# The shift of the first score tiles, added by VectorE out of PSUM instead of by ScalarE and GpSimd

## Chip, cores and metric

The kernel runs on one core of one Trainium2 chip. The metric is the device time of one execution in microseconds (us). TensorE does the matrix products, ScalarE (ACT) the exponentials and many copies, VectorE (DVE) and GpSimd (POOL) elementwise work, SyncE (SP) issues the DMAs.

## What is computed

Two independent blocks on 2048 tokens of width 448, side by side in the output:

```python
# block A: real part of a two-dimensional DFT by matrices
a = einsum("bsd,ed->bse", x, dft_hid_re);  b = einsum("bsd,ed->bse", x, dft_hid_im)
yA = einsum("ts,bse->bte", dft_seq_re, a) - einsum("ts,bse->bte", dft_seq_im, b)
# block B: attention with 16 heads of 28
q, k, v = split(x @ wqkv);  p = softmax(q @ k.T * 28**-0.5);  yB = concat_heads(p @ v) @ wo
out = concatenate([yA, yB], axis=-1)
```

All data are float32. Products whose precision matters are done in three parts: each factor is split into a rounded high part (type float32r) and the remainder, the low part, and high × high, low × high and high × low are summed in PSUM.

## The kernel before

**Work.** Block B first projects x to Q, K and V: chains of 11 matmuls (three row blocks of 128 with three products each, and a last one with two), 28 chains for Q and K (`project`, line 622, with 512 columns) and 16 for V (`values`, line 652, with 448). The results go out to DRAM: for Q and K as a high and a low part (`stored`, line 590: ACT copies the high part out of the PSUM bank at line 593, VectorE subtracts the low part at line 594), for V by a VectorE copy (line 667). Block A has two parts, real and imaginary. Each has 16 hidden products (`hidden`, line 678, again chains of 11 matmuls, with the high part copied by ACT at line 689 or 693 and the low part taken by VectorE at line 690 or 695) and 16 sequence products of 192 matmuls (`sequence`, line 700). The matrices for them come in pieces: ACT rounds the high part (line 520), POOL subtracts the low part (line 526).

Attention runs head by head, with keys on the partitions: per head 16 key tiles × 4 chunks of 512 queries. A score matmul (line 862) writes a PSUM bank, ACT takes the exponential into a kept tile (line 866), and after every 8 key tiles one group of products with V (line 844; 32 products, 64 matmul records) adds them up. 

**The shift.** No running maximum is kept. Instead a shift per query is found from the first key tile of each head (`first_tiles`, line 788): four score matmuls (line 800), copied out by ACT (line 804); VectorE transposes them in blocks of 32 (line 805), takes maxima (806 to 820) and leaves the negated shift in `am`, 64 values wide, with the query of a block on the partitions. Then, for each of the four chunks, VectorE transposes `am`, broadcast, into a PSUM bank (line 826). ACT copies that bank to the SBUF tile `mb`, rounded to float32r (line 829). POOL copies one row of `mb` into row 96 of the chunk's Q tile (line 830), so that the score matmuls of the other key tiles add the shift by themselves, and POOL adds `mb` to the first tile's scores (line 832). ACT then takes their exponential (line 834). So every score matmul at line 862 waits for its chunk's row.

**PSUM.** Of the 8 banks, 2 (`fill_s`) serve the chains of projections and of block A; 6 (`bank_s`) serve scores, transposes, the shift and the sums over V.

**Kept tiles.** `kept_s` has 20 pairs (`NKEPT`) of 128 × 512 float32. A pair holds exponentials until their group of products with V has run; the projections' and block A's results pass through pairs too. Three more pairs are lent where the weights of block A are not in use.

**Order.** Every engine executes its instructions in a fixed order, which is planned when the program is written out (`Schedule`, line 173). Each step has a key, roughly the time in us when it is due, the steps it depends on and the buffers it needs. The planner walks through time with its own prices for every step; an engine that is free takes the ready step with the lowest key. The argument `soon` lowers the key:

```python
t.engs, t.key, t.emit, t.lat, t.lock, t.mode = engs, key - soon, emit, lat, lock, mode   # line 188
```

`SOON` is 40. Before, the rounding of a piece (line 520) and the high copy of a hidden product (689, 693) have it; the high copy of a projection (593) has not, and has the key of its chain less 10, while an exponential has the key of its score matmul less 20. The keys of the heads run evenly from 56 to 935 us (`T_ATT`, `T_END`), those of the other matrix work, the filler, evenly to 1005 us (`T_FILL`), and TensorE interleaves the two by key. The first tiles of a head have keys that begin 26 before the head's.

**End.** After the last head's products with V its sums are normalised by way of DRAM (`out_of`, line 873). The output projection (line 984) follows; what is left of the filler covers the time between.

Of the kernel before, what the change touches and what calls it, by code (L numbers as in the profile page):

```python
# [11 lines left out]
F32 = mybir.dt.float32  # L12
F32R = mybir.dt.float32r
AF = mybir.ActivationFunctionType
ALU = mybir.AluOpType
# [9 lines left out]
P = 128  # L25
NT = S // P
CH = 512
# [3 lines left out]
SCALE = DH ** -0.5  # L31

KM = 98
NKEPT = 20
NKEYS = 5
NFILL = 2
Q_YO = 2
# [3 lines left out]
SOON = 40.0  # L41
# [7 lines left out]
def f32(ap):  # L49
    return ap.bitcast(F32)  # L50
# [275 lines left out]
def tile_kernel(ctx, tc, xa, wre, wim, wd, xb, wqkv, wo, out):  # L326
    nc = tc.nc
# [7 lines left out]
    def new(name, shape, dtype=F32, n=None, in_turn=False, space=None):  # L335
        if space is DRAM:
            return dram.tile(shape, dtype, name=name)
        if n is None:
            return sb.tile(shape, dtype, tag=name, name=name)
        sch.pools.append(Slots([sb.tile(shape, dtype, tag=f"{name}{i}", name=f"{name}{i}") for i in range(n)], in_turn))  # L340
        return sch.pools[-1]
# [18 lines left out]
    v_s = new("v", [P, NC, 4, VW], F32, 2, True)  # L360
    q_s = new("q", [P, CH], F32R, 8, True)
    kept_s = new("kept", [P, 2, CH], F32, NKEPT)
    mb_s = new("mb", [P, CH], F32R, 2, True)
    sm_s = new("sm", [P, 2, NT], F32, 2)
    qm_s = new("qm", [P, 4, 4 * NT], F32, 2, True)
    am_s = new("am", [P, 4 * NT], F32, 2, True)
    ok = new("ok", [P, 2 * H], F32)
    banks = [ps.tile([P, CH], F32, tag=f"bank{i}", name=f"bank{i}") for i in range(8)]

# [4 lines left out]
    fill_s, bank_s = Slots(banks[:NFILL]), Slots(banks[NFILL:])  # L374
# [36 lines left out]
    def act(key, emit, d=ACT_P, **kw):  # L411
        return sch.add({"ACT": d}, key, lambda e: emit(), **kw)

    def dve(key, emit, d=DVE_P, **kw):
        return sch.add({"DVE": d}, key, lambda e: emit(), **kw)

    def pool(key, emit, d=POOL_2, **kw):
        return sch.add({"POOL": d}, key, lambda e: emit(), **kw)
# [171 lines left out]
    def stored(j, c, o, end, own, hi, lo, st, key, out_key):  # L590
        cols = slice(c * CH, (c + 1) * CH)
        as_r, as_f = (lambda t: t if st else f32r(t)), (lambda t: f32(t) if st else t)
        a = act(key, lambda: nc.scalar.activation(as_r(hi.t), o.t, AF.Copy), deps=[end], use=[o, *own])
        b = dve(key, lambda: nc.vector.tensor_tensor(as_r(lo.t), o.t, as_f(hi.t), op=ALU.subtract), deps=[a], use=[o, *own])  # L594
        qk_done[j, c] = [
            dma(out_key, lambda: nc.sync.dma_start(f32(qk_d[j * P:(j + 1) * P, 0, cols]), as_f(hi.t)), deps=[a], use=own),
            dma(out_key, lambda: nc.sync.dma_start(f32(qk_d[j * P:(j + 1) * P, 1, cols]), as_f(lo.t)), deps=[b], use=own)]
# [54 lines left out]
    def values(ready, chunks):  # L652
        for c in chunks:
            v_done[c] = []
            for t in range(4):
                tok = slice(c * CH + t * P, c * CH + (t + 1) * P)
                o, pair = fill_s.slot(), kept_s.slot()
                vs = Half(pair, 0)
                seq = products(lambda k: lz(x_h, k, tok), lambda k: lz(x_l, k, tok), lambda: lz(x_3, tok),
                               lambda k: (lambda: w_first.h[:, k]), lambda k: (lambda: w_first.l[:, k]))  # L660
                key = fkey(11, M448)
                end = chain(key, seq, o, D, [], [], M448, [pair],
                            {3 * k: [xb_ready[c, k], ready[k], *ready[4:][:k // 3]] for k in range(4)}, v_last)

                def put(o=o, vs=vs):
                    v3 = vs.t.rearrange("p (h d) -> p h d", h=H)
                    nc.vector.tensor_copy(v3[:, :, :DH], o.t[:, :D].rearrange("p (h d) -> p h d", h=H))
                    nc.vector.memset(v3[:, :, DH:DH + 1], 1.0)
                    nc.vector.memset(v3[:, :, DH + 1:], 0.0)
                b = dve(key - 20, put, 0.85, deps=[end], use=[o, pair])  # L670
                v_done[c].append(dma(key - 20, lambda vs=vs, c=c, t=t: nc.sync.dma_start(
                    v_d[:, :, (4 * c + t) * VW:(4 * c + t + 1) * VW].rearrange("h p x -> p h x"),
                    vs.t.rearrange("p (h x) -> p h x", h=H)), extra=1.0, deps=[b], use=[pair]))
# [83 lines left out]
    KT, VT, Q = {}, {}, {}  # L757
# [27 lines left out]
    R = {}  # L785
    checked = []

    def first_tiles(h):

        qm, am = qm_s.slot(), am_s.slot()  # L790
        Q[h] = [q_s.slot() for c in range(NC)]
        pairs = [kept_s.slot() for _ in range(NC // 2)]
        R[h] = {0: [Half(pairs[c // 2], c % 2) for c in range(NC)]}
        key0 = begins[h] - 26
        made, rs = [], []
        for c in range(NC):
            key = key0 + 2 * c
            q, s, o, tm = Q[h][c], R[h][0][c], bank_s.slot(), bank_s.slot()
            lq = load_q(h, c, q)
            m = pe(key, lambda e, o=o, q=q: nc.tensor.matmul(  # L800
                o.t, KT[h][0].t[:KR, :P], q.t[:KR, :], start=True, stop=True),
                deps=[*lq, *got_k[h, 0], before.get("f")], use=[o, s.pair, q, KT[h][0], tm])
            in_line("f", m)
            made.append(act(key, lambda o=o, s=s: nc.scalar.activation(s.t, o.t, AF.Copy), deps=[m], use=[o, s.pair], lock=[o]))  # L804
            t = dve(key, lambda o=o, tm=tm: nc.vector.transpose(tm.t, o.t), 0.66, deps=[m], use=[o, tm], lock=[o], own=RAW_S)  # L805
            rs.append(dve(key, lambda tm=tm, c=c: nc.vector.tensor_reduce(  # L806
                qm.t[:, 0, c * NT:(c + 1) * NT], tm.t.rearrange("p (j r) -> p j r", r=32), axis=AX.X, op=ALU.max, negate=True),
                0.64, deps=[t], acq=[qm] if c == 0 else [], use=[tm] if c == 0 else [tm, qm], own=RAW_S))
        key = key0 + 8

        def beside(i):
            return lambda: nc.vector.tensor_copy(qm.t[:32, i, :], qm.t[32 * i:32 * i + 32, 0, :])  # L812

        def back(n):
            return lambda: nc.vector.tensor_copy(am.t[n:2 * n, :], am.t[:n, :])
        r = [dve(key, beside(i), SMALL, deps=rs, use=[qm]) for i in (1, 2, 3)]
        r = dve(key, lambda: nc.vector.tensor_reduce(  # L817
            am.t[:32, :], qm.t[:32].rearrange("p i x -> p x i"), axis=AX.X, op=ALU.min), 0.4,
            deps=r, acq=[am], use=[qm])
        for n in (32, 64):  # L820
            r = dve(key, back(n), SMALL, deps=[r], use=[am])
        row, shown = [], []
        for c in range(NC):
            key = key0 + 10 + 2 * c
            q, s, pm, mb = Q[h][c], R[h][0][c], bank_s.slot(), mb_s.slot()
            t = dve(key, lambda pm=pm, c=c: nc.vector.transpose(  # L826
                pm.t, am.t[:, c * NT:(c + 1) * NT].unsqueeze(2).to_broadcast([P, NT, 32])), 0.64,
                deps=[r], acq=[pm], use=[am])
            ld = act(key, lambda pm=pm, mb=mb: nc.scalar.activation(mb.t, pm.t, AF.Copy), deps=[t], acq=[mb], use=[pm])  # L829
            row.append(pool(key, lambda q=q, mb=mb: nc.gpsimd.tensor_copy(q.t[96:97, :], mb.t[96:97, :]), 0.7,  # L830
                            deps=[ld], use=[mb, q]))
            sh = pool(key, lambda s=s, mb=mb: nc.gpsimd.tensor_tensor(s.t, s.t, f32(mb.t), op=ALU.add), deps=[ld, made[c]],  # L832
                      use=[s.pair, mb])
            shown.append(act(key, lambda s=s: nc.scalar.activation(s.t, s.t, AF.Exp, scale=SCALE), ACT_S, deps=[sh], use=[s.pair]))  # L834
        return row, shown

# [62 lines left out]
    o = bank_s.slot()  # L899
# [18 lines left out]
    key = fkey(0, 0)  # L918
    staged = [d for j in range(N_FIRST, 5) for c in range(NC) for d in qk_done[j, c]]
    made = hidden(0, w_first, load_w(w_first, lambda k: wd[:, k, :D], key - 10, after=[v_last[0], *staged]), x_users)  # L920
# [3 lines left out]
    key = fkey(0, 0)  # L924
    w_b = Weights(lent)
    lent.until.append(key - 50)
    made = hidden(1, w_b, load_w(w_b, lambda k: wd[:, k, D:], key - 10, after=[a_last]), [y_last])
# [12 lines left out]
    for n, c in enumerate(range(NC)):  # L940
        raws = []
        for k in range(4):
            pair = kept_s.slot()
            raw = Half(pair, 0)
            key = T_OUT + n
            deps = [o_done[h, c] for h in range(H) if (h + 1) * DH > k * P and h * DH < (k + 1) * P] + [before["k"]]
            if k < 3:
                ld = dma(key, lambda raw=raw, k=k, c=c: nc.sync.dma_start(raw.t, on_d[k * P:(k + 1) * P, c * CH:(c + 1) * CH]),
                         deps=deps, use=[pair])
            else:  # L950
# [3 lines left out]
                ld = dma(key, twice, 128, n=2, deps=deps, use=[pair])  # L954
            raws.append((raw, ld))
        for i in range(2):
            x = [q_s.slot() for _ in range(4)]
            ready = []
            for k in range(4):
                raw, ld = raws[k]  # L960
# [148 lines left out]
```

## Time and profile before

| | us |
|---|---|
| median of 3 runs | 1024.51 (1023.98 to 1025.2) |
| the profiled execution | 1024.84, span 1022.9 |
| TensorE busy | 1010.6 (99%) |
| ACT busy | 742.3 (73%) |
| POOL busy | 405.6 (40%) |
| VectorE busy | 280.5 (27%) |
| granted TensorE clock | 0.999 of full speed |

A row of a group of instructions reads: line, engine, operation, output <- inputs, shapes, count, then busy us, mean ns of one, and the idle time of the engine just before them with what ended it. A row of the timeline reads: start in us, length in us, engine, line, operation, count, and in brackets the idle time before it and its releaser. A row of the chain of waits has start, length and the piece of work. PE is TensorE's matmuls, PEld its weight loads.

### The profile page before, as it was taken

How to read it: one execution, taken by the hardware profiler on the slowest of the kernel's cores; microseconds unless marked ns; L12 is line 12 of the kernel's file. 1: busy time of each engine (PE TensorE's matmuls, PEld its weight loads, DVE VectorE, ACT ScalarE, POOL GpSimd, SP SyncE). 2: the span in 40 equal slices, each digit the busy share in tenths (PEclk: the TensorE clock that was granted, in tenths of full speed). 3: DMA queues.
4: the chain of work that ended last, by engine and by line, in shares of the span. 5: the costliest groups of instructions: out<-in, count | busy, mean ns of one | idle time of the engine just before them, and what ended most of it. 6: DMA issues, size and time to landing. Idle time of an engine off the chain costs nothing.

```text
span 1022.9 us, 16066 instructions
## 1 busy us (share of the span) xinstructions
PE 1010.6 (99%) x5634; PEld 730.5 (71%) x5634; DVE 280.5 (27%) x542; ACT 742.3 (73%) x1471; POOL 405.6 (40%) x410
## 2 busy tenths in 40 slices
PE   8999999999999999999999999999999999999997
PEld 7885667776666676767767776666676767777896
DVE  6351415241403122131313141503113131300212
ACT  6137879878787878686878878787868687977232
POOL 7021332444352525253534535352535253553530
PEclk9999999999999999999999999999999999999999
DMA  9795464314242323333332424233424334243732
GB/s 322 219 164 159 153 198 136 111 51 124 73 123 83 109 88 114 94 103 104 110 105 84 132 84 114 74 113 99 127 94 130 104 110 122 76 136 101 218 126 92
DMA packets 109909, 124.84 MB, mean 122 GB/s; under 512 B 48640, under 2 KB 61440, under 8 KB 109824
## 3 DMA queue, kind: packets, MB, share of 16 engines
q1 hardware_dynamic: 109824, 123.78, 40.5%
q8 instruction: 45, 0.74, 0.3%
q14 instruction: 40, 0.33, 0.1%
HBM read 89.92 MB, written 33.69 MB: 121 GB/s over the span
## 4 chain that ended last, share of the span: by engine, by line
PE 93%; DVE 3%; ACT 2%; DMA 1%; issue 1%; SPq 0%; DVEq 0%; ACTq 0%
PE bank L714 30%; PE bank L844 22%; PE bank L862 22%; PE bank L577 15%; PE bank L984 4%; PE bank L800 1%; ACT kept L866 1%; DVE big L423 1%; DMA kept<-wqkv 1%; DMA kept<-xb 0%; DVE bank L826 0%; DVE qm L812 0%; ACT kept L804 0%; DVE kept L594 0%; DVE am L817 0%
## 5 line engine op out<-in xcount | busy, mean ns | idle before, releaser
L866 ACT ACTIVATE kept<-bank 128x512 f32<-128x512 f32 x958 | 520.0, 670 | 84.1 <-PE bank L862 75.5
L526 POOL TENSOR_TENSOR wlo<-wraw,whi 128x512 fp32r<-128x512 f32 (+1 forms) x164 | 201.8, 1231 | 437.4 <-ACT whi L520 363.9
L862 PE MATMUL bank<-q,k 98*128 98x512 f32 x960 | 339.1, 401 | 1.6 <-ACT kept L866 1.2
L714 PE MATMUL bank<-big,whi 128*128 128x448 f32 x1024 | 316.3, 368 | 0.0
L844 PE MATMUL bank<-kept,v 128*32 128x512 f32 x2044 | 226.4, 594 | 0.0
L862 PEld LDWEIGHTS bank<-q,k 98*128 98x128 f32 x960 | 179.9, 188 | 55.0 <-ACT kept L866 8.5
L714 PEld LDWEIGHTS bank<-big,whi 128*128 128x128 f32 x1024 | 193.1, 189 | 31.1 <-issue 7.5
L714 PE MATMUL bank<-big,wlo 128*128 128x448 f32 x512 | 188.3, 368 | 0.0
L844 PEld LDWEIGHTS bank<-kept,v 128*32 128x32 f32 x2044 | 63.3, 110 | 144.7 <-issue 142.0
L520 ACT ACTIVATE whi<-wraw 128x512 fp32r<-128x512 f32 x164 | 113.9, 695 | 26.9 <-PE bank L714 20.0
L714 PEld LDWEIGHTS bank<-big,wlo 128*128 128x128 f32 x512 | 96.7, 189 | 15.8 <-issue 5.0
L805 DVE STREAM_TRANSPOSE bank<-bank 128x512 f32<-128x512 f32 x64 | 46.7, 730 | 205.3 <-PE bank L800 158.4
L832 POOL TENSOR_TENSOR kept<-kept,mb 128x512 f32<-128x512 f32 x64 | 82.3, 1286 | 5.1
L577 PE MATMUL bank<-wd,whi 128*128 128x448 f32 x256 | 80.3, 367 | 0.8 <-DVE big L690 0.7
L834 ACT ACTIVATE kept<-kept 128x512 f32<-128x512 f32 x64 | 44.5, 701 | 42.5 <-POOL kept L832 42.5
L830 POOL CAST q<-mb 1x512 fp32r<-1x512 f32 x64 | 38.9, 608 | 90.5 <-ACT mb L829 88.1
L804 ACT ACTIVATE kept<-bank 128x512 f32<-128x512 f32 x64 | 41.5, 653 | 42.3 <-PE bank L800 40.8
L577 PE MATMUL bank<-big,whi 128*128 128x512 f32 x175 | 60.1, 396 | 1.5 <-DVE kept L594 1.2
L577 PEld LDWEIGHTS bank<-wd,whi 128*128 128x128 f32 x256 | 48.3, 189 | 7.7 <-DVE big L690 1.1
L772 DVE TENSOR_REDUCE ok<-v 128x1 f32<-128x512 f32 x16 | 11.0, 686 | 141.0 <-DMA v<-vd 141.0
L829 ACT ACTIVATE mb<-bank 128x512 fp32r<-128x512 f32 x64 | 42.3, 723 | 5.6 <-DVE bank L826 5.5
L806 DVE TENSOR_REDUCE qm<-bank 128x16 f32<-128x512 f32 x64 | 44.0, 688 | 1.9
(74 smaller groups left out, 707.4 us busy)
## 6 DMA issues: line engine op xcount, KB each, us to landing
wraw<-wre SPq DMA_DIRECT2D x64, 256.0 KB
wraw<-wim SPq DMA_DIRECT2D x64, 256.0 KB
qkd<-kept SPq DMA_DIRECT2D x40, 256.0 KB
wraw<-xa SPq DMA_DIRECT2D x32, 256.0 KB
k<-qkd SPq DMA_DIRECT2D x64, 112.0 KB
q<-qkd SPq DMA_DIRECT2D x64, 112.0 KB
out<-kept SPq DMA_DIRECT2D x32, 224.0 KB
kept<-xb SPq DMA_DIRECT2D x16, 256.0 KB
```

Source lines behind the costliest of these rows:

```text
L520: a = act(key + (0 if early else 1), lambda: nc.scalar.activation(self.hi.t, raw.t, AF.Copy), ACT_S, soon=SOON, deps=[ld], acq=[self.hi], ...
L526: b = sch.add(e, at, lambda g: eng[g].tensor_tensor(self.lo.t[:, :n], raw.t[:, :n], f32(self.hi.t)[:, :n], op=ALU.subtract), deps=[a], acq ...
L577: nc.tensor.matmul(o.t[:, :cols], w(), x(), start=(i == 0), stop=(i == n - 1))
L714: nc.tensor.matmul(o.t[:, :D], a.t[:, k, :], b[:, q * 4 + k, :], start=(q == 0 and k == 0 and j == 0), stop=(q == 3 and k == 3 and j == 2))
L805: t = dve(key, lambda o=o, tm=tm: nc.vector.transpose(tm.t, o.t), 0.66, deps=[m], use=[o, tm], lock=[o], own=RAW_S)
L806: rs.append(dve(key, lambda tm=tm, c=c: nc.vector.tensor_reduce(qm.t[:, 0, c * NT:(c + 1) * NT], tm.t.rearrange("p (j r) -> p j r", r=32), ...
L829: ld = act(key, lambda pm=pm, mb=mb: nc.scalar.activation(mb.t, pm.t, AF.Copy), deps=[t], acq=[mb], use=[pm])
L832: sh = pool(key, lambda s=s, mb=mb: nc.gpsimd.tensor_tensor(s.t, s.t, f32(mb.t), op=ALU.add), deps=[ld, made[c]], use=[s.pair, mb])
L834: shown.append(act(key, lambda s=s: nc.scalar.activation(s.t, s.t, AF.Exp, scale=SCALE), ACT_S, deps=[sh], use=[s.pair]))
L844: nc.tensor.matmul(o.t[c * VW:(c + 1) * VW, :], VT[h].t[:, kt // 4, kt % 4, :], tiles[kt][c].t, start=(kt == 0), stop=(kt == NT - 1))
L862: m = pe(key, lambda e, o=o, q=q, kt=kt: nc.tensor.matmul(o.t, KT[h][kt // 4].t[:KM, kt % 4 * P:(kt % 4 + 1) * P], q.t[:KM, :], start=True ...
L866: es.append(act(key - 20, lambda o=o, p=p: nc.scalar.activation(p.t, o.t, AF.Exp, scale=SCALE), deps=[m], use=[o, p.pair]))
```

## The change

1. `am` becomes float32r, so the shift is rounded in the 64 wide reduction that makes it. The transposed shift in PSUM needs no rounding copy after that: the ACT copy to `mb`, and `mb` itself, are dropped.
2. The row of Q is copied out of PSUM by VectorE instead of out of `mb` by POOL.
3. The shift is added to the first tile's scores by VectorE, straight from PSUM, instead of by POOL from `mb`.
4. `NKEPT` is 21 instead of 20; `mb` had two tiles of 128 × 512, which is the size of a pair.
5. The high copy of a projection out of its bank gets `soon=SOON`, and the copy of a V projection out of its bank gets a key lower by 25.

```diff
-NKEPT = 20
+NKEPT = 21
...
-    mb_s = new("mb", [P, CH], F32R, 2, True)
...
-    am_s = new("am", [P, 4 * NT], F32, 2, True)
+    am_s = new("am", [P, 4 * NT], F32R, 2, True)
...
-        a = act(key, lambda: nc.scalar.activation(as_r(hi.t), o.t, AF.Copy), deps=[end], use=[o, *own])
+        a = act(key, lambda: nc.scalar.activation(as_r(hi.t), o.t, AF.Copy), deps=[end], use=[o, *own], soon=SOON)
...
-                b = dve(key - 20, put, 0.85, deps=[end], use=[o, pair])
+                b = dve(key - 45, put, 0.85, deps=[end], use=[o, pair])
...
-            q, s, pm, mb = Q[h][c], R[h][0][c], bank_s.slot(), mb_s.slot()
+            q, s, pm = Q[h][c], R[h][0][c], bank_s.slot()
             t = dve(key, lambda pm=pm, c=c: nc.vector.transpose(
-                pm.t, am.t[:, c * NT:(c + 1) * NT].unsqueeze(2).to_broadcast([P, NT, 32])), 0.64,
+                pm.t, f32(am.t)[:, c * NT:(c + 1) * NT].unsqueeze(2).to_broadcast([P, NT, 32])), 0.64,
                 deps=[r], acq=[pm], use=[am])
-            ld = act(key, lambda pm=pm, mb=mb: nc.scalar.activation(mb.t, pm.t, AF.Copy), deps=[t], acq=[mb], use=[pm])
-            row.append(pool(key, lambda q=q, mb=mb: nc.gpsimd.tensor_copy(q.t[96:97, :], mb.t[96:97, :]), 0.7,
-                            deps=[ld], use=[mb, q]))
-            sh = pool(key, lambda s=s, mb=mb: nc.gpsimd.tensor_tensor(s.t, s.t, f32(mb.t), op=ALU.add), deps=[ld, made[c]],
-                      use=[s.pair, mb])
+            row.append(dve(key, lambda q=q, pm=pm: nc.vector.tensor_copy(q.t[96:97, :], pm.t[96:97, :]), 0.55, deps=[t], use=[pm, q]))
+            sh = dve(key, lambda s=s, pm=pm: nc.vector.tensor_tensor(s.t, s.t, pm.t, op=ALU.add), deps=[t, made[c]], use=[s.pair, pm])
```

The numbers 0.64, 0.55 and the like are the planner's prices in us; the add is planned at 0.60.

## The prediction

> **What bounds the kernel now.** I read the page's busy times first, then the stretches, then the chain of waits, then the timeline around each place where TensorE starts a matmul late, and last the groups of instructions for prices.
>
> ```profile
> span 1022.9 us, 16066 instructions
> PE 1010.6 (99%) x5634; PEld 730.5 (71%) x5634; DVE 280.5 (27%) x542; ACT 742.3 (73%) x1471; POOL 405.6 (40%) x410
> ```
>
> TensorE is busy 99% of the span. Of the engines the change touches, ACT has 73%, POOL 40%, VectorE 27%. "Busy" is modelled from pipelined matmuls, so I also want the rate at which they start:
>
> ```profile
> 937.24 0.93 PE bank L862 x4
> 950.62 28.57 PE bank L714 x140
> 979.19 35.90 PE bank L984 x176
> 1015.09 1.45 PE bank L714 x7
> ```
>
> In these pieces of the chain of waits a 448-column matmul costs 28.57/140 = 0.204 us and a 512-column one 0.93/4 = 0.233 us. A matmul that starts later than this after the one in front has lost time, even where the row shows no idle time.
>
> The Trainium skill ("Perfetto Trace Analysis", Identifying the Most-Contended Engine) says that matmul busy time is a poor measure and that weight-load busy time should be used; by its 71% TensorE would have room. The trace does not bear this out here: 147 matmuls of one line run at 0.204 to 0.207 us with no release from another engine between them, so in this program weight loads hide under matmuls.
>
> Where is time lost?
>
> ```profile
> 60.00:310.00 250.00, 247.28 (x1361) 173.09 (x1360) 80.33 (x162) 199.60 (x397) 95.40 (x104) 1.00 0.45 129
> 310.00:600.00 290.00, 289.89 (x1682) 203.20 (x1681) 70.67 (x130) 221.86 (x438) 117.85 (x106) 1.00 0.34 101
> ```
>
> The columns are TensorE, weight load, VectorE, ACT, POOL busy. From 310 to 600 us TensorE stands 0.1 us; from 60 to 310 us it stands 2.7 us, and there ACT is busy 80%. That early stretch has the projections and the first hidden products, whose chains of 11 matmuls alternate between two PSUM banks. So the change can only win what is lost there (and in the second hidden stage near 610 us); elsewhere less work on ACT or POOL is worth nothing. I looked at each late start:
>
> ```profile
> 85.53 4.21 ACT L866 ACTIVATE kept<-bank 128x512 f32<-128x512 f32 x8
> 87.01 3.29 PE L862 MATMUL bank<-q,k 98*128 98x512 f32 x9
> 89.34 0.89 ACT L593 ACTIVATE wd<-bank 128x512 fp32r<-128x512 f32 x1
> 90.33 0.69 DVE L594 TENSOR_TENSOR wd<-bank,wd 128x512 fp32r<-128x512 f32 x1 [10.08 <-ACT wd L593]
> 90.78 0.51 PE L862 MATMUL bank<-q,k 98*128 98x512 f32 x1 [0.48 <-ACT kept L866]
> ...
> 109.33 0.86 PE L862 MATMUL bank<-q,k 98*128 98x512 f32 x3
> 110.42 0.73 PE L577 MATMUL bank<-big,whi 128*128 128x512 f32 x2 [0.23 <-DVE wd L594]
> ...
> 64.72 3.84 PE L577 MATMUL bank<-wd,big 128*128 128x448 f32 x18
> 68.96 1.09 PE L577 MATMUL bank<-wd,big 128*128 128x448 f32 x4 [0.40 <-DVE kept L667]
> ...
> 221.21 1.91 DVE L826 STREAM_TRANSPOSE bank<-am 128x512 f32<-128x512 f32 x3
> 222.33 0.78 PE L577 MATMUL bank<-wd,whi 128*128 128x448 f32 x3
> 223.15 0.63 DVE L690 TENSOR_TENSOR big<-bank,big 128x448 fp32r<-128x448 f32 x1
> 223.83 0.47 PE L577 MATMUL bank<-wd,whi 128*128 128x448 f32 x1 [0.73 <-DVE big L690]
> ...
> 276.66 2.51 DVE L826 STREAM_TRANSPOSE bank<-am 128x512 f32<-128x512 f32 x4
> 277.42 0.60 ACT L829 ACTIVATE mb<-bank 128x512 fp32r<-128x512 f32 x1 [0.49 <-DVE bank L826]
> 277.95 0.37 PE L714 MATMUL bank<-big,whi 128*128 128x448 f32 x1
> 278.15 0.61 POOL L830 CAST q<-mb 1x512 fp32r<-1x512 f32 x1 [2.72 <-ACT mb L829]
> 278.56 0.51 PE L862 MATMUL bank<-q,k 98*128 98x512 f32 x1 [0.24 <-ACT kept L866]
> ...
> 117.97 1.22 PE L862 MATMUL bank<-q,k 98*128 98x512 f32 x3
> 119.02 0.63 PE L577 MATMUL bank<-big,whi 128*128 128x512 f32 x2
> ...
> 616.55 1.44 PE L862 MATMUL bank<-q,k 98*128 98x512 f32 x3
> 617.83 0.37 PE L577 MATMUL bank<-wd,whi 128*128 128x448 f32 x1
> ```
>
> Start to start, less the pitch: (a) 87.01 to 90.78 is 3.77 for nine, less 9 × 0.233 = 2.10: 1.67 lost. TensorE had only score matmuls to run, at the pace of the exps, because the projection bank was not copied out: the copy L593 stood on ACT behind eight exps. (b) 109.33 to 110.42: 1.09 − 0.70 = 0.39, again released by L594 behind L593. (c) 64.72 to 68.96: 4.24 − 18 × 0.204 = 0.57, released by the value copy L667. (d) 222.33 to 223.83: 1.50 − 0.61 = 0.89; the low half L690 stood behind three transposes. (e) 277.95 to 278.56: 0.61 − 0.20 = 0.41; the first score matmul of a head waits for the shift's row to pass VectorE, ACT and POOL. (f) Five more (the first and last are shown: 1.05 − 0.70 = 0.35 and 1.28 − 0.70 = 0.58), where ACT is behind with exps or with copies, 2.2 together. Sum: 1.67 + 0.39 + 0.57 + 0.89 + 0.41 + 2.2 = 6.1 us. That is what there is to win.
>
> **The change part by part.**
>
> ```profile
> L829 ACT ACTIVATE mb<-bank 128x512 fp32r<-128x512 f32 x64 | 42.3, 723 | 5.6 <-DVE bank L826 5.5
> L830 POOL CAST q<-mb 1x512 fp32r<-1x512 f32 x64 | 38.9, 608 | 90.5 <-ACT mb L829 88.1
> L832 POOL TENSOR_TENSOR kept<-kept,mb 128x512 f32<-128x512 f32 x64 | 82.3, 1286 | 5.1
> L826 DVE STREAM_TRANSPOSE bank<-am 128x512 f32<-128x512 f32 x64 | 41.4, 700 | 2.2 <-ACT kept L866 0.4
> L594 DVE TENSOR_TENSOR kept<-bank,kept 128x512 fp32r<-128x512 f32 x20 | 13.5, 689 | 27.9 <-ACT kept L593 27.7
> L667 DVE COPY kept<-bank 128x448 f32<-128x448 f32 x16 | 9.9, 620 | 19.4 <-PE bank L577 19.3
> ```
>
> *Removed.* 64 ACT copies: 42.3 us of ACT, so 742.3 becomes about 700. 64 casts and 64 adds of POOL: 38.9 + 82.3 = 121.2 us, so 405.6 becomes about 284. Neither engine ends the span; ACT's 2.6 us a head matter only in the early stretch.
>
> *Added.* 64 adds on VectorE with one operand in PSUM: the nearest row is L594, 0.689 us. 64 row copies of one partition by 512 out of PSUM: the nearest is L667, 0.620 at 448 columns, and L594 is the upper bound at 512; I take 0.69, as time follows columns and not partitions. 64 × (0.69 + 0.69) = 88 us: VectorE goes to about 369 us, 36%. Between independent instructions less than this passes: four transposes of 0.70 take 2.51, so they start every 0.60. The bounds of the added occupation are thus 77 and 88 us, hidden behind TensorE unless a low half queues behind it.
>
> The Trainium skill ("VectorE: DVE Perf Modes", The DRAIN you can't avoid) states that the next VectorE instruction does not start until the pipe is empty. By that the four transposes would take 2.80 us; the trace's 2.51 says they overlap by 0.10 each. By the rule the chain for a head would be 8.3 us, which the bound from durations has already.
>
> *The latency of the shift.* Before, from the first transpose to the end of the first row: 276.66 to 278.15 + 0.61 = 278.76, 2.10 us over three engines. After: 0.70 + 0.69 = 1.39 on one. (e) goes: next late is the K or q load, of which the trace shows no wait there. A whole head's chain is 4 × (0.70 + 0.69 + 0.69) = 8.3 us of VectorE where the transposes alone took 2.51. The bank that holds the shift is freed after some 2.1 us and no longer waits for ACT's turn. Rounding while 64 wide changes one reduction's output type: nothing, as it is the same instruction on the same columns.
>
> *Precedence on ACT.* The copy L593 gets a key 40 lower, so it passes queued exps. For (a) it would run at the start of the run of eight exps instead of behind it: the next chain starts in time, and 1.67 goes; for (b) 0.39. Behind it on ACT the exps wait one copy longer, 0.5 us, which six score banks cover. The rows of the first three projections already had the smallest keys; nothing changes there.
>
> *Precedence of the value copies* on VectorE: (c), 0.57, goes. Behind it waits the shift of head 0, some 0.6 us longer for each copy; TensorE has value matmuls to run meanwhile (18 in a row above).
>
> *One more pair.* Two more tiles of exps can be held while a group of products with V runs; where TensorE doesn't stand (310 to 600) this is worth nothing, early on a part of (f). A loss would need the planner's order to worsen; I take nothing.
>
> *The end.* From the last product with V at 950.62 TensorE has 28.57 us of sequence matmuls, then the output's 176, then 1.45 us of leftover. If attention ended later against the filler by more than 1.45 us, the output's normalisation would be exposed. The keys hold the two in step, so I take 0.
>
> *Sum.* Gone: (a) + (b) + (c) + (e) = 3.04. Of (d) and (f), 3.1 us, I take half, 1.55: ACT is lighter, but a low half can now also stand behind an add or a row. New collisions: the first tiles of seven heads fall in stages with 11-matmul chains; at one collision in every seven or eight of 0.89 as in (d), 0.9 us. 3.04 + 1.55 − 0.9 = 3.7 us. The profiled execution took 1024.84 with a span of 1022.9 and lies 0.3 above the median of 1024.51; a saving is the same in both. 1024.5 − 3.7 = 1020.8.
>
> **The rivals.**
>
> *VectorE in the way* (slower). VectorE works strictly in its planned order. In each of seven heads its busy stretch grows from 2.5 to 8.3 us while low halves (L594, L690, L695) must go out every chain, 11 × 0.204 = 2.25 us at the fastest. If the planner places a row and an add ahead of a low half that is in fact ready, TensorE stands as in (d). From 4.6/0.89, five such collisions on top, the gain is gone; at nine more, 8.0 − 4.6 = 3.4 us are lost: about 1028. For it: (d) itself, where three transposes were enough. Against it: low halves have earlier keys than the shift's steps, so the planner lets one pass between two of them, and a step is only 0.7 us.
>
> *The stalls only move* (same). The order is fixed by the planner's own prices, which may see no queue at 85 us at all, so that the precedence changes nothing there, and (a) stays or another copy is late. Then (c), (e) and half of (d) and (f) less the 0.9 remain: 0.57 + 0.41 + 1.55 − 0.9 = 1.6, 1022.9. This is also the case in which the change doesn't do what it says.
>
> *ACT had been the bound* (much faster). Were TensorE not full, 42.3 us less of ACT, the next busiest, could shorten everything: towards 1024.5 − 42 = 982. The stretch from 310 to 600 us, with TensorE without a gap and ACT busy 221.86 of 290, speaks against it. (This is what the Trainium skill's weight-load rule, in "Perfetto Trace Analysis", Identifying the Most-Contended Engine, would point to.)
>
> **How the numbers follow.** Forecast 0.60 (1018.4 with all 6.1 gone, to 1022.4 with 2.1), only moved 0.20, VectorE in the way 0.19, ACT 0.01. The range, 1017 to 1027, takes in the forecast's own and the moved case and half of the slower one; its lower end allows 1.4 us for gaps too small to be listed. About 0.2%, 2 us, is what a measurement can tell from no change: faster 0.61, same 0.20, slower 0.19.
>
> **What would show it.** VectorE about 369 us, ACT about 700, POOL about 284; the row copy and the add about 0.69 us each; no run of nine score matmuls near 87 us, and L593 ahead of the exps; no wait of TensorE for L667; the first scores of a head 0.7 us sooner. From 60 to 310 us TensorE busy above 248.5. Wrong: TensorE waits for L594, L690 or L695 behind adds in more than four places, or a gap between 950 and 980 us.

## The result: 1040.45 us, slower by 1.6%

| kernel | median us | ratio to before, 95% interval |
|---|---|---|
| before | 1024.51 | |
| after | 1040.45 | 1.0158 [1.0146, 1.0170] |

The forecast was 1020.8, faster. The change cost 15.9 us. In the kernel after, line numbers lie one lower up to the shift and four lower behind it: score matmul 858 (before 862), exp 862 (866), products with V 840 (844), transpose of the shift 825 (826). The new row copy is 828, the new add 829. The page of the profile after:

```profile
span 1038.6 us, 15903 instructions
PE 1016.1 (98%) x5634; PEld 733.9 (71%) x5634; DVE 369.8 (36%) x670; ACT 713.1 (69%) x1407; POOL 285.0 (27%) x282
L830 ACT ACTIVATE kept<-kept 128x512 f32<-128x512 f32 x64 | 39.3, 640 | 15.2 <-DVE kept L829 15.2
L828 DVE CAST q<-bank 1x512 fp32r<-1x512 f32 x64 | 44.6, 697 | 2.4
```

VectorE and POOL have the work that was forecast (369.8 and 285.0 us; a row copy takes 0.697). ACT is lighter, though it has 713.1 us where about 700 was forecast. And yet the span is 15.7 us longer. The stretches (TensorE, weight load, VectorE, ACT, POOL busy) say where:

```profile
60.00:310.00 250.00, 246.54 (x1355) 171.56 (x1354) 108.71 (x202) 190.59 (x378) 57.61 (x64) 1.00 0.44 128
310.00:600.00 290.00, 285.94 (x1654) 198.81 (x1652) 95.44 (x165) 207.79 (x408) 78.73 (x64) 1.00 0.32 100
```

From 310 to 600 us, where TensorE had stood 0.1 us before and I had ruled out that anything mattered, it now stands 4.1 us. From 60 to 310 us, where more than 248.5 us busy was forecast, it has 246.54. The waits of the kernel after name the releaser (total us, times, longest):

```profile
PEld bank L858 <- DVE kept L829: 28.1, 37, 1.5
PE bank L858 <- DVE kept L829: 13.6, 25, 1.1
PE bank L576 <- DVE kept L593: 0.4, 1, 0.4
```

Score matmuls wait for the add. The nearest in the profile before are 2.0 us for POOL's add and 1.8 us for ACT's copy, both on the weight loads alone. One head on the timeline:

```profile
328.33 1.19 DVE L811 COPY qm<-qm 32x64 f32<-32x64 f32 x3
329.56 0.61 DVE L816 TENSOR_REDUCE am<-qm 32x64 fp32r<-32x256 f32 x1
330.20 0.41 DVE L814 CAST am<-am 32x64 fp32r<-32x64 f32 x2
330.72 0.73 DVE L825 STREAM_TRANSPOSE bank<-am 128x512 f32<-128x512 f32 x1
331.48 0.70 DVE L828 CAST q<-bank 1x512 fp32r<-1x512 f32 x1
331.68 0.57 PE L713 MATMUL bank<-big,whi 128*128 128x448 f32 x2
332.19 0.69 DVE L829 TENSOR_TENSOR kept<-kept,bank 128x512 f32<-128x512 f32 x1
332.79 0.72 DVE L825 STREAM_TRANSPOSE bank<-am 128x512 f32<-128x512 f32 x1
332.93 0.51 PE L858 MATMUL bank<-q,k 98*128 98x512 f32 x1 [0.67 <-DVE kept L829]
...
336.49 0.37 PE L713 MATMUL bank<-big,whi 128*128 128x448 f32 x1
337.07 0.50 PE L858 MATMUL bank<-q,k 98*128 98x512 f32 x1 [0.21 <-DVE kept L829]
```

The score matmul at 332.93 starts 0.05 us behind the end of the add (332.88). Start to start, TensorE loses 1.25 − 0.41 = 0.84 and 0.58 − 0.20 = 0.38 here, 1.2 us in this head. Reckoned in the same way over the whole trace, score matmuls start late behind an add in 15 of the 16 heads (all but the first), 0.55 to 1.9 us in each and about 19 us together. That covers the 15.9 us lost and leaves room for what the change wins elsewhere.

The planner had these steps at other prices. From the first of the three copies (811) to the first transpose: 3 × 0.21 + 0.40 + 2 × 0.21 = 1.45 planned, 330.72 − 328.33 = 2.39 measured (1.76 to 3.31 over the 16 heads). A chunk's transpose, row and add: 0.64 + 0.55 + 0.60 = 1.79 planned, 332.79 − 330.72 = 2.07 measured. So the first chunk's bank comes 0.94 + 0.28 = 1.2 us later than planned and the fourth's 2.1. TensorE works through a fixed order, in which a score matmul stands at the planned moment of the release.

### The profile page after: what moved, and what is told of

It is laid out like the page before. It is cut to its first block, busy times and chain, and to the rows that moved or that the text cites. A ratio compares the mean times of both kernels' runs of the same rounds, so it can differ in the third digit from the quotient of the medians.

```text
span 1038.6 us, 15903 instructions
## 1 busy us (share of the span) xinstructions
PE 1016.1 (98%) x5634; PEld 733.9 (71%) x5634; DVE 369.8 (36%) x670; ACT 713.1 (69%) x1407; POOL 285.0 (27%) x282
## 4 chain that ended last, share of the span: by engine, by line
PE 82%; DVE 13%; ACT 2%; issue 1%; DMA 1%; SPq 0%; DVEq 0%; ACTq 0%
PE bank L713 24%; PE bank L840 22%; PE bank L858 17%; PE bank L576 13%; PE bank L980 3%; DVE kept L829 3%; DVE bank L825 3%; DVE q L828 3%; ACT kept L862 2%; PE bank L799 1%; DVE qm L811 1%; DVE bank L804 1%; DVE qm L805 1%; PE bank L611 1%; DVE am L814 1%
## 5 line engine op out<-in xcount | busy, mean ns | idle before, releaser
L858 PE MATMUL bank<-q,k 98*128 98x512 f32 x960 | 335.0, 402 | 14.4 <-DVE kept L829 13.6
L713 PE MATMUL bank<-big,whi 128*128 128x448 f32 x1024 | 313.1, 369 | 0.0
L519 ACT ACTIVATE whi<-wraw 128x512 fp32r<-128x512 f32 x164 | 108.0, 658 | 27.5 <-PE bank L713 22.5
L830 ACT ACTIVATE kept<-kept 128x512 f32<-128x512 f32 x64 | 39.3, 640 | 15.2 <-DVE kept L829 15.2
L825 DVE STREAM_TRANSPOSE bank<-am 128x512 f32<-128x512 f32 x64 | 46.1, 720 | 1.7
L828 DVE CAST q<-bank 1x512 fp32r<-1x512 f32 x64 | 44.6, 697 | 2.4
```

The costliest lines, as they stand in the source:

```text
L519: a = act(key + (0 if early else 1), lambda: nc.scalar.activation(self.hi.t, raw.t, AF.Copy), ACT_S, soon=SOON, deps=[ld], acq=[self.hi], ...
L713: nc.tensor.matmul(o.t[:, :D], a.t[:, k, :], b[:, q * 4 + k, :], start=(q == 0 and k == 0 and j == 0), stop=(q == 3 and k == 3 and j == 2))
L825: t = dve(key, lambda pm=pm, c=c: nc.vector.transpose(pm.t, f32(am.t)[:, c * NT:(c + 1) * NT].unsqueeze(2).to_broadcast([P, NT, 32])), 0.6 ...
L828: row.append(dve(key, lambda q=q, pm=pm: nc.vector.tensor_copy(q.t[96:97, :], pm.t[96:97, :]), 0.55, deps=[t], use=[pm, q]))
L858: m = pe(key, lambda e, o=o, q=q, kt=kt: nc.tensor.matmul(o.t, KT[h][kt // 4].t[:KM, kt % 4 * P:(kt % 4 + 1) * P], q.t[:KM, :], start=True ...
```

## The experiments

The theories: **late chain** (the prices are too low, so the order on TensorE is too early for what VectorE does), **banks** (the shift's banks are missing to the scores, whatever the price), **precedence** (copies pushed ahead hold up the exps). And within the first: is it the bank or the row in Q that the score matmuls stand for? Each ratio is to the kernel before as it was measured beside that run, at a median of 1024.44 to 1024.59 us.

| run | median us | ratio to before, 95% interval |
|---|---|---|
| e1 chain alone | 1044.23 | 1.0190 [1.0173, 1.0207] |
| e2 precedence alone | 1022.30 | 0.9972 [0.9961, 0.9984] |
| e3 new steps priced | 1027.38 | 1.0024 [1.0013, 1.0036] |
| e4 all priced | 1016.69 | 0.9921 [0.9904, 0.9937] |
| e5 shift in SBUF | 1020.09 | 0.9955 [0.9939, 0.9972] |
| e6 bank later | 1020.65 | 0.9964 [0.9952, 0.9977] |
| e7 row later | 1040.62 | 1.0157 [1.0140, 1.0174] |
| e8 before, priced | 1019.18 | 0.9949 [0.9932, 0.9966] |
| e9 priced, 20 pairs | 1016.67 | 0.9917 [0.9900, 0.9933] |
| e10 priced, no precedence | 1022.05 | 0.9973 [0.9963, 0.9984] |
| e11 overpriced | 1019.13 | 0.9945 [0.9928, 0.9962] |

**e1, the chain alone.** Against the kernel after:

```diff
-NKEPT = 21
+NKEPT = 20
-        a = act(key, lambda: nc.scalar.activation(as_r(hi.t), o.t, AF.Copy), deps=[end], use=[o, *own], soon=SOON)
+        a = act(key, lambda: nc.scalar.activation(as_r(hi.t), o.t, AF.Copy), deps=[end], use=[o, *own])
-                b = dve(key - 45, put, 0.85, deps=[end], use=[o, pair])
+                b = dve(key - 20, put, 0.85, deps=[end], use=[o, pair])
```

> Only the shift's move to VectorE (and the earlier rounding); kept pairs 20, no new precedence. Theory 'late chain' (the planner's prices for the shift's steps on VectorE are too low, 1.79 us a chunk against 2.07 measured and 1.45 us for the six small steps before it against 2.39; so score matmuls stand on TensorE behind a PSUM bank that the add frees up to 2 us later than planned, about 1 us in each of 16 heads): 1038 to 1044 us, TensorE's wait for the add at least 12 us. Theory 'banks' (the shift simply occupies banks that the scores need, whatever the prices): the same 1038 to 1044. Theory 'precedence' (projection copies pushed ahead hold up the exps): about 1024.

Its TensorE waits:

```profile
PE bank L858 <- DVE kept L829: 13.7, 27, 1.1
```

At 1044.23 the loss is whole, larger than with the rest, and 0.2 us above the range that two of the theories had given: the move to VectorE is the cause, precedence is not. Whether it is the late chain or the banks, this run doesn't tell.

**e2, precedence alone.** The same two edits of keys, made on the kernel before.

> The kernel before with only the two precedences (high copy of a projection 40 earlier, value copy 25 earlier); the shift still goes by ACT and POOL, 20 pairs. 'Late chain' and 'banks': 1020 to 1024, and the run of nine score matmuls near 87 us is gone. 'Precedence': about 1038.

The copies out of a projection bank, and the longest run of score matmuls from 83 to 92 us, on its timeline:

```profile
84.62 0.75 ACT L593 ACTIVATE wd<-bank 128x512 fp32r<-128x512 f32 x1
85.48 0.69 DVE L594 TENSOR_TENSOR wd<-bank,wd 128x512 fp32r<-128x512 f32 x1 [6.44 <-ACT wd L593]
87.94 0.95 PE L862 MATMUL bank<-q,k 98*128 98x512 f32 x3
```

The copy that stood behind eight exps at 89.34 now starts at 84.62, and the run of nine score matmuls is gone. 2.3 us are won (1024.59 in the kernel before beside it).

**e4, all steps priced.** The program does the same work as the kernel after; only the planner's numbers differ.

```diff
-                0.64, deps=[t], acq=[qm] if c == 0 else [], use=[tm] if c == 0 else [tm, qm], own=RAW_S))
+                0.70, deps=[t], acq=[qm] if c == 0 else [], use=[tm] if c == 0 else [tm, qm], own=RAW_S))
-        r = [dve(key, beside(i), SMALL, deps=rs, use=[qm]) for i in (1, 2, 3)]
+        r = [dve(key, beside(i), 0.40, deps=rs, use=[qm]) for i in (1, 2, 3)]
-            am.t[:32, :], qm.t[:32].rearrange("p i x -> p x i"), axis=AX.X, op=ALU.min), 0.4,
+            am.t[:32, :], qm.t[:32].rearrange("p i x -> p x i"), axis=AX.X, op=ALU.min), 0.64,
-            r = dve(key, back(n), SMALL, deps=[r], use=[am])
+            r = dve(key, back(n), 0.26, deps=[r], use=[am])
...
-                pm.t, f32(am.t)[:, c * NT:(c + 1) * NT].unsqueeze(2).to_broadcast([P, NT, 32])), 0.64,
+                pm.t, f32(am.t)[:, c * NT:(c + 1) * NT].unsqueeze(2).to_broadcast([P, NT, 32])), 0.76,
-            row.append(dve(key, lambda q=q, pm=pm: nc.vector.tensor_copy(q.t[96:97, :], pm.t[96:97, :]), 0.55, deps=[t], use=[pm, q]))
+            row.append(dve(key, lambda q=q, pm=pm: nc.vector.tensor_copy(q.t[96:97, :], pm.t[96:97, :]), 0.71, deps=[t], use=[pm, q]))
-            sh = dve(key, lambda s=s, pm=pm: nc.vector.tensor_tensor(s.t, s.t, pm.t, op=ALU.add), deps=[t, made[c]], use=[s.pair, pm])
+            sh = dve(key, lambda s=s, pm=pm: nc.vector.tensor_tensor(s.t, s.t, pm.t, op=ALU.add), 0.62, deps=[t, made[c]], use=[s.pair, pm])
```

> The changed kernel with nothing but the planner's prices of the shift's steps set to what its trace shows (transpose 0.76, row 0.71, add 0.62, the small steps 0.40, 0.64, 0.26, the maxima 0.70). 'Late chain': at most 1026, TensorE's wait for the add below 3 us. 'Banks' and 'precedence': 1036 to 1041, as the work is the same.

Its stretch and all of its TensorE waits:

```profile
310.00:600.00 290.00, 290.00 (x1681) 206.56 (x1674) 99.20 (x172) 212.52 (x421) 80.86 (x68) 1.00 0.32 101
PE bank L900 <- POOL ident masks.py:199: 1.4, 1, 1.4
PE bank L576 <- DVE kept L593: 1.3, 2, 1.0
PE bank L611 <- ACT big L485: 0.9, 1, 0.9
```

The wait for the add is gone from TensorE, and so are 23.8 us against the kernel after. The steps themselves take as long as in the kernel after:

```profile
L828 DVE CAST q<-bank 1x512 fp32r<-1x512 f32 x64 | 44.6, 697 | 2.4
L829 DVE TENSOR_TENSOR kept<-kept,bank 128x512 f32<-128x512 f32 x64 | 44.0, 687 | 1.1
```

That refutes "banks" as well: the shift holds its banks as long as in the kernel after (2.3 us on average in both), but TensorE has filler to do meanwhile, once the order says so. (A sequence product of the filler has 4 × 12 = 48 matmuls, not the 192 that the section on the kernel before gives.) This version beats both kernels, the one before by 0.8%.

**e3, only the new steps priced.** The last three edits of e4 (transpose, row, add); the steps ahead keep their prices.

> The changed kernel with only the three new steps priced as measured (transpose 0.76, row 0.71, add 0.62); the six small steps before them keep their low prices. 'Late chain' says lateness adds up: 0.9 us from the small steps and 0.28 more with each chunk, so this takes away about two fifths to a half of the loss of 24 us against the fully priced kernel: 1022 to 1033. If the new steps alone are the cause: 1016 to 1019. If the small steps alone: 1037 or more.

```profile
PE bank L858 <- DVE kept L829: 5.5, 9, 0.9
```

1027.38, with 5.5 us of these waits left on TensorE. 13.1 of the 23.8 us are gone, a little more than the half that was worked out at most: the lateness adds up over both parts.

**e6 and e7, bank or row.** The planner is told that the one or the other comes 1.5 us later, and nothing else (`lat` is the planner's delay from a step's end to its release, 0.15 otherwise; in e7 the bank is left out of the row's list, so that the row's delay doesn't hold it in the plan).

```diff
# e6
-            sh = dve(key, lambda s=s, pm=pm: nc.vector.tensor_tensor(s.t, s.t, pm.t, op=ALU.add), deps=[t, made[c]], use=[s.pair, pm])
+            sh = dve(key, lambda s=s, pm=pm: nc.vector.tensor_tensor(s.t, s.t, pm.t, op=ALU.add), lat=1.65, deps=[t, made[c]], use=[s.pair, pm])
# e7
-            row.append(dve(key, lambda q=q, pm=pm: nc.vector.tensor_copy(q.t[96:97, :], pm.t[96:97, :]), 0.55, deps=[t], use=[pm, q]))
+            row.append(dve(key, lambda q=q, pm=pm: nc.vector.tensor_copy(q.t[96:97, :], pm.t[96:97, :]), 0.55, lat=1.65, deps=[t], use=[q]))
```

> The changed kernel at its own low prices, but the planner is told that what the add releases (its PSUM bank, its kept pair, the exp behind it) comes 1.5 us later; the row in Q is as before. If the score matmuls stand for the bank: at most 1022, wait for the add below 4 us. If they stand for the row: 1036 or more.

> The reverse of the run beside it: the planner is told that the row in Q comes 1.5 us later, the bank's release is as in the changed kernel. If the score matmuls stand for the bank: 1034 or more, wait for the add still at least 10 us. If for the row: at most 1024.

TensorE's waits for the add, first in e6, then in e7:

```profile
PE bank L858 <- DVE kept L829: 1.4, 5, 0.3
...
PE bank L858 <- DVE kept L829: 14.3, 27, 1.1
```

It is not the row: a delay planned for it changes nothing (1040.62), one planned for what the add releases wins 19.8 us. What the add releases is the bank, the first tile's pair and the exp behind it, and e6 delays the three together; e5 singles out the bank.

**e5, the shift in SBUF.** The transposes write two SBUF tiles, so no bank is taken; prices as in the kernel after.

```diff
-NKEPT = 21
+NKEPT = 20
+mb_s = new("mb", [P, CH], F32, 2, True)
-q, s, pm = Q[h][c], R[h][0][c], bank_s.slot()
+q, s, pm = Q[h][c], R[h][0][c], mb_s.slot()
```

> The changed kernel with the transposed shift written to two SBUF tiles instead of to PSUM banks, at unchanged prices (20 pairs, since the tiles take the room of one). If the score matmuls wait for the bank ('late chain' by way of the bank, or 'banks'): 1020 to 1030, wait for the add gone. If they wait for the shift's row in Q ('late chain' by way of the row): 1034 or more, waits at the row copy. 'Precedence': about 1038.

1020.09, and no row of a wait for the add (here line 830). The row copy also got cheaper (below), so that this head's first chunk takes 327.60 − 325.79 = 1.81 us, close to the planned 1.79:

```profile
325.79 0.71 DVE L826 STREAM_TRANSPOSE mb<-am 128x512 f32<-128x512 f32 x1
326.53 0.42 DVE L829 CAST q<-mb 1x512 fp32r<-1x512 f32 x1
326.99 0.69 DVE L830 TENSOR_TENSOR kept<-kept,mb 128x512 f32<-128x512 f32 x1
327.60 0.70 DVE L826 STREAM_TRANSPOSE mb<-am 128x512 f32<-128x512 f32 x1
```

But that is one of the quickest chunks. Over the run, the three steps are hardly shorter than in the kernel after:

```profile
L826 DVE STREAM_TRANSPOSE mb<-am 128x512 f32<-128x512 f32 x64 | 45.0, 703 | 0.5
L829 DVE CAST q<-mb 1x512 fp32r<-1x512 f32 x64 | 34.4, 538 | 2.4
```

With 0.819 us for the add (its row stands in the last section) their means make 2.06 us, against 0.720 + 0.697 + 0.687 = 2.10 in the kernel after, and both are planned at 1.79. VectorE is thus about as late against the plan as before, and TensorE doesn't wait, since no bank hangs on it.

**e8, the control without the move.** e2 with the first four edits of e4, those ahead of the transposes of `am`; ACT and POOL carry the shift.

> Control without the move: the kernel before with both precedences and with the small steps ahead of the shift priced as measured (0.70, 0.40, 0.64, 0.26); ACT and POOL carry the shift. If the move itself is worth something at right prices: 1019 to 1023, near the 1022.3 of precedence alone. If the right prices are all there is to the 1016.7: at most 1018.

1019.18: right prices for the small steps are worth 3.1 us also where the shift isn't moved. The steps of ACT and POOL keep their prices here, which are close to their rows (a row copy planned at 0.70 and 0.608 measured, an add at 1.25 and 1.286). What the move itself is worth is then 1019.18 − 1016.69 = 2.5 us.

**e9, e10, e11, on top of e4.** In e9 `NKEPT` is 20; in e10 the two edits of keys in e1 are made; e11 has prices too high by as much as they had been too low:

```diff
-0.70 (maxima), 0.40 (beside), 0.64 (to am), 0.26 (back), 0.76 (transpose), 0.71 (row), 0.62 (add)
+0.76 (maxima), 0.59 (beside), 0.88 (to am), 0.31 (back), 0.88 (transpose), 0.87 (row), 0.64 (add)
```

> The fully priced kernel (1016.7) with 20 kept pairs instead of 21. If the pair is worth nothing, as predicted for where TensorE doesn't stand: 1016 to 1018. If it carries the gain over precedence alone: 1019 or more.

> The fully priced kernel without the two precedences (21 pairs). By the prediction's items (a), (b) and (c) they are worth up to 2.6 us; alone on the kernel before they gave 2.2: 1018 to 1020. If lighter ACT has made them idle: 1016 to 1017.

> The fully priced kernel with the same steps priced too high by as much as they had been too low (transpose 0.88, row 0.87, add 0.64, maxima 0.76, small steps 0.59, 0.88, 0.31). By 'late chain' only the too low side costs TensorE time, since it works on the filler when a bank comes early: 1016 to 1019. If what helped was a hit on one lucky order: anywhere, above 1022 or so.

The pair is worth nothing (1016.67). The precedences are worth 5.4 us, more than either expectation had it: in e10 the value copies and the longer chain of head 0 meet on VectorE, and TensorE waits there (the middle row is a wait for exps on ACT). The three rows make 3.4 of the 5.4 us:

```profile
PE bank L858 <- DVE q L828: 1.5, 1, 1.5
PE bank L858 <- ACT kept L862: 1.1, 2, 0.9
PE bank L576 <- DVE kept L666: 0.8, 1, 0.8
```

Overpricing costs 2.4 us (0.1 more than the range allowed), underpricing by as much had cost 23.8. That speaks against e4 as a lucky order; the two sides of a wrong price differ tenfold.

## Why the prediction was wrong

*The step that failed* is the shift's latency, in its effect on TensorE. The prediction has the added 77 to 88 us of VectorE "hidden behind TensorE unless a low half queues behind it", and says of the bank only that it "is freed after some 2.1 us and no longer waits for ACT's turn". No term of the sum stands for score matmuls that wait for this bank. The runs show that wait in its place: TensorE stands 13.6 us for the add in the kernel after; 23.8 us go when the steps are priced as measured (e4), and the wait goes when the shift takes no bank (e5).

The durations were right: the chain of a head on VectorE, 8.3 us (in the head above the last add ends at 339.62, which makes 8.9 with a copy of another step, 0.54, in between), and the bank's hold (330.72 to 332.88, 2.16). But I set these against what the same steps took before, not against what the planner believed of them. With planned 1.79 a chunk beside my own 2.07 the lateness could have been worked out from the kernel's text and the rows at hand. I also took the bank's shorter hold for a help: shorter it is (2.25 us on average over the 64 banks, from the transpose's start to the end of the last reader, against 6.8 before), but TensorE's order presumes an even shorter one. "A loss would need the planner's order to worsen; I take nothing" was said of the extra pair alone, which e9 bears out; for the steps of the shift I never asked it.

*Why it hadn't shown before* is argued and not run. Then the bank was released by ACT's copy. The price of the transposes was right for four in a row, which start every 0.60. The small steps were too cheap already, which e8 puts at 3.1 us.

*The stretch that I ruled out.* "Elsewhere less work on ACT or POOL is worth nothing" was right for less work; I read it as if nothing could be lost there either. 310 to 600 us alone lost 4 us of TensorE.

*The slower rival* had the sign and the engine, not the place: low halves behind adds. TensorE's waits for L593 in the kernel after are 0.4 us, and none for 689 or 694 are listed. Its point of decision, five collisions, never came up (on top of the forecast, which has one collision in it already, it would be 3.7/0.89, about four); the heads lost about 1 us each by another wait.

*Two readings that don't hold.* (e) was put down to the shift's row. But the line shown names ACT's exp (L866) as the releaser, and the score matmul starts at 278.56, ahead of the row's end at 278.76; among TensorE's matmuls before, none is listed as waiting for L830. And the 2.10 us for the first row before is the shortest of the 16 heads; the median is 2.79.

*What was right.* (a) and (b): the copies ahead of the exps; with (c) they were put at 2.6, and e2 gave 2.3, but in e10 against e4 5.4, so this term was undersized on the changed kernel. The latency of the row: the first one is done 1.46 us behind the start of its transpose (1.39 forecast). The extra pair, put at next to nothing, is worth nothing. A gain like the forecast's 3.7 us is there once the prices are right: 7.9 in e4, of which e8 puts 3.1 on prices that help without the move too, so 4.8. No run splits it into the terms of the forecast.

*Sizes.* ACT fell by 29 us and not by 42.3. The busy time of a row counts its overlap with neighbours on the same engine; 64 copies at the 0.50 us from start to start (277.42 to 277.92 in the trace before) make 32, an estimate from one copy. VectorE, POOL, row and add came out within about 1%.

*The pipe.* In a chunk of the kernel after, a row behind its transpose and an add behind the row start 0.76 and 0.71 us later, without overlap; only the next transpose starts 0.60 behind the add, and the chunk takes 2.07. The Trainium skill's rule of the drain ("VectorE: DVE Perf Modes", The DRAIN you can't avoid) gives 0.73 + 0.70 + 0.69 = 2.12 us, so here it was nearer than three times the 0.60 from four transposes, 1.80. The same section adds that a next instruction that is not held starts earlier. My reading, that independent instructions are the ones that overlap, doesn't hold: the add needs nothing from the row, and still starts only behind its end. What separates the two cases no run here shows.

## What to carry to other kernels

Where the order of every engine is fixed in advance from prices, an edit that moves a step to another engine also moves it to another price: compare the planned duration with the row of the trace, and sum the difference along the chain up to the resource that the bound engine is queued for. Here prices that were too low stalled the bound engine (23.8 us), and prices as much too high mostly made it do something else first (2.4 us). And a stretch in which the bound engine never waits has nothing to win from lighter neighbours, but it can still lose.

## What the runs showed of the hardware

Two things from e5 against the kernel after, and what the second means for the prices. A row of 512 float32 that VectorE copies takes 0.42 us out of SBUF (0.538 on average, as 15 of the 64 start beside an instruction of POOL and take longer) and 0.697 out of PSUM. The Trainium skill ("VectorE: DVE Perf Modes", The perf-mode tier table, with Why PSUM operands drop a tier) has it so: twice the rate for a float32 copy within SBUF, and none of that with an operand in PSUM.

And the add with both inputs in SBUF takes 0.69 us alone and 1.75 beside POOL's subtraction, while the add out of PSUM has a mean of 0.687 over the run:

```profile
661.81 1.29 POOL L526 TENSOR_TENSOR wlo<-wraw,whi 128x512 fp32r<-128x512 f32 x1 [2.54 <-ACT whi L520]
661.90 1.75 DVE L830 TENSOR_TENSOR kept<-kept,mb 128x512 f32<-128x512 f32 x1
...
L830 DVE TENSOR_TENSOR kept<-kept,mb 128x512 f32<-128x512 f32 x64 | 52.4, 819 | 4.1 <-ACT kept L804 2.5
```

The add starts 0.09 us behind POOL's instruction and ends 0.55 us behind its end, nearly as if it had begun then. So do all ten of the 64 adds that start during an instruction of POOL (0.55 us behind its end each); the other 54 take about 0.69. The Trainium skill ("SBUF — State Buffer", SBUF: two separate sides) states just this: a VectorE instruction with two SBUF inputs and a GpSimd instruction that reads SBUF take the shared ports one after the other. So keeping the shift in PSUM, as the change does, spares VectorE this wait, at the price of a bank.

The small steps ahead of the shift wait for POOL in a similar way. In the head of the kernel after that is shown above, the first of the three copies at 811 reads:

```profile
327.79 1.29 POOL L525 TENSOR_TENSOR wlo<-wraw,whi 128x512 fp32r<-128x512 f32 x1 [2.58 <-ACT whi L519]
328.33 0.79 DVE L811 COPY qm<-qm 32x64 f32<-32x64 f32 x1
```

It ends 0.04 us behind POOL's subtraction, where the next one takes 0.18 us in all. Of the 80 copies at 811 and 814, 16 start during an instruction of POOL, and each ends 0.04 to 0.05 us behind it. So 0.6 of the 0.94 us by which this head's small steps came late is time spent waiting for POOL. The 0.40 us at which e4 prices such a copy is a third of this head's 1.19 us, with the wait in it; over the run the mean of one is 0.305.
